# Four weight units of a mixer converted during attention, on one Trainium2 core

## The chip, the cores and the metric

One core of one Trainium2 chip runs the whole program. The metric is the device time of one execution in microseconds (us), as the median of several runs. The engines named below are PE (TensorE matmul), DVE (VectorE), ACT (ScalarE), POOL (GpSimd) and SP, which here only issues DMAs.

## What is computed

A clustered attention (2 batches, 8 heads, 768 positions, 64 wide; a query sees a key only if both fall to the same of 16 centroids of its head) feeds two mixers in a row:

```python
x = attention(q, k, v, centroids)              # 2 x 768 x 512
u = x + (x^T @ U @ V)^T                        # first mixer, rank 32
x = u + relu(u @ w_ch1) @ w_ch2                # w_ch1 512 x 2048, w_ch2 2048 x 512
h = relu(x^T @ w_tok1) @ w_tok2                # second mixer
u = x + h^T
out = u + relu(u @ w_ch1') @ w_ch2'            # 1536 wide
```

The weights arrive as 64-bit floats and are used as a pair of 32-bit parts (a high one that the fast matmul takes exactly, and the rest), so each product is three matmuls.

## The kernel before

**Attention** runs in 96 steps (function step, lines 643 to 693), one tile of 128 queries each. Step n issues the score matmuls of tile n+2, DVE's maximum over them (s_max, line 289), ACT's exponential of tile n+1 (s_exp, line 294), PE's transposes of tile n (line 311), their copies out of PSUM by ACT and DVE in turn (lines 318 and 316), and the product with v. Other work is hung on steps by two tables: mid, which runs before the exponential, and late, which runs at the end of the step. The late table holds the preparation of the next pair of heads: at step s1-8 its load, at s1-5 to s1+2 its scores, the cluster choice (arg0, arg2 and arg4 on DVE, arg1, arg3, k_lo and mask_rows on POOL, q_lo on DVE), where s1 is a multiple of 12. PE's transposes and several small products share three PSUM banks in turn (ring, line 301).

**Units.** The first mixer's channel weights come as NFA = 16 units of 1 MB of 64-bit numbers (a slice of w_ch1 and one of w_ch2). The function wide (line 490) converts unit k in stages numbered d: 1 loads it (SP, line 494), 3 takes the magnitude (ACT, line 96), 4, 4.5, 5 and 5.5 are four DVE operations on 1024 columns (lines 100, 103, 106, 109), 6 rounds the high part (ACT), 6.5 subtracts for the low part (DVE for the first ND = 6 units, POOL for the others), and 7 stores 1 MB to a scratch array in DRAM (SP, line 513 or 522). Two raw buffers alternate, so the load of a unit waits for stage 5.5 of the unit two before it.

**The schedule of the conversion.** Units 0 to 3 begin during attention, by the hand-written table early (line 628). The rest runs in ticks: tick n does stage d of unit k where 2k + int(d) = n (conv_all, line 555); after the 16 units follow 31 smaller blocks (narrow) for the second mixer.

**The mixer** runs in slots (half_slots, line 797). Slot 2k+1 issues hidden(k+1), 12 matmuls of 512 columns with the first half of a unit, slot 2k+2 issues outmm(k), 12 with the second half; between them ACT and DVE make gh and gl (lines 728 and 729). Each unit serves four passes over the tokens, the first two interleaved by the cuts 0, 6, 11, 16: units 0 to 5 for pass 0, then for pass 1, then units 6 to 10 for both, then 11 to 15. The weights stand in three buffers (whl), and the function feed (line 704) fetches a half (512 KB) from the scratch array, for every place from the seventh on, four slots before its use: slot 2u-5 fetches the first half for place u, used in slot 2u-1, and slot 2u-2 the second half, used in slot 2u+2. Below, F12 is the fetch issued in slot 12.

Before each slot the main loop steps two generators, rest_of_u and conv_rest (line 894); the latter decides whether the slot gets a tick:

```python
if k + NTICK < 2 * ND + 5 or k % 9 % 2 or k % 9 == 0:
    tick()
```

so slots 0 to 7 have one tick each, and from slot 8 on five slots of nine have one (9, 10, 12, 14, 16, 18, 19, 21, 23 and so on). All loads, stores and fetches are issued by SP in the order in which the program names them, and one that has to wait holds back those behind it.

Of the kernel before, what the change touches and what calls it, by code (L numbers as in the profile page):

```python
# [10 lines left out]
F32R = mybir.dt.float32r  # L11
# [7 lines left out]
P = 128  # L19
# [5 lines left out]
def tile_cluster_attention__then__two_mixers(  # L25
# [32 lines left out]
    NFA, NFB = wa.shape[0], wb.shape[0]  # L58
# [25 lines left out]
    def sub(eng, o, a, b):  # L84
        eng.tensor_tensor(out=o, in0=a, in1=b, op=ALU.subtract)  # L85
# [3 lines left out]
    def conv(dst, raw):  # L89


        w = raw.bitcast(I32).rearrange("p (n two) -> p n two", two=2)
        lo, hi, d = w[:, :, 0], w[:, :, 1], dst.bitcast(I32)

        def magnitude():
            act.activation(dst, hi.bitcast(F32), AF.Abs)  # L96

        def clamp():

            dve.tensor_scalar(out=dst, in0=dst, scalar1=2.0 ** -15, scalar2=122879.9921875, op0=ALU.max, op1=ALU.min)  # L100

        def shift():
            dve.tensor_scalar(out=d, in0=d, scalar1=3, scalar2=0x3FFFFFF8, op0=ALU.logical_shift_left, op1=ALU.bitwise_and)

        def low_bits():
            dve.scalar_tensor_tensor(out=d, in0=lo, scalar=29, in1=d, op0=ALU.logical_shift_right, op1=ALU.bitwise_or)  # L106

        def top_bits():
            dve.scalar_tensor_tensor(out=d, in0=hi, scalar=-0x40000000, in1=d, op0=ALU.bitwise_and, op1=ALU.bitwise_or)  # L109

        return [magnitude, clamp, shift, low_bits, top_bits]
# [5 lines left out]
    ND = cuts[1]  # L117
# [13 lines left out]
    w64 = [c64_[:, ts(i, 1024)] for i in range(2)]  # L131
    w32 = [c32_[:, ts(i, 1024)] for i in range(2)]
    u0 = [qk0[:, ts(i, 2048)].rearrange("p (c n) -> p c n", c=NC) for i in range(2)]
    chl = [qk1[:, ts(4 + i, 1024)].rearrange("p (h n) -> p h n", h=2) for i in range(2)]
# [3 lines left out]
    ap = ap_ctx.enter_context(tc.tile_pool(name="ap", bufs=1))  # L138
# [22 lines left out]
    pt = ap.tile([P, 4 * NBL * P], F32, name="pt")  # L161
    osb = [ap.tile([P, HS], F32, name=f"osb{i}") for i in range(2)]
    nm = ap.tile([P, 4], F32, name="nm")
    rs = [ap.tile([P, 2 * NT], F32, name=f"rs{i}") for i in range(4)]
    rr = [ap.tile([P, 2 * NT], F32, name=f"rr{i}") for i in range(2)]

# [315 lines left out]
    blocks = []  # L482
# [4 lines left out]
            blocks.append((wt2[ts(c, P), ts(h, HS)].unsqueeze(1), None, (c, h)))  # L487
    blocks += [(wb[f][:, ts(i, 512)], scr[1][f, i], None) for f in range(NFB) for i in range(2)]

    def wide(k, d):  # L490
        r64, r32 = w64[k % 2], w32[k % 2]
        ops = conv(r32, r64)
        if d == 1:
            sp.dma_start(r64, wa[k])
        elif d == 3:
            ops[0]()
        elif d == 4:
            ops[1]()
        elif d == 4.5:
            ops[2]()  # L500
        elif d == 5:
            ops[3]()
        elif d == 5.5:
            ops[4]()
        elif k < ND:
            o, r = whl[k % NW], r32.rearrange("p (i n) -> p i n", i=2)
            if d == 6:
                rnd(act, o[:, :, 0, :], r)
            elif d == 6.5:
                sub(dve, o[:, :, 1, :], r, f32(o[:, :, 0, :]))  # L510
            else:
                for i in range(2):
                    sp.dma_start(scr[0][k, i], f32(o[:, i]).rearrange("p h n -> p (h n)"))
        else:
            for i in range(2):
                o, r = chl[2 * (k % 2) + i], r32[:, ts(i, 512)]
                if d == 6:
                    rnd(act, o[:, 0, :], r)
                elif d == 6.5:
                    sub(pool, o[:, 1, :], r, f32(o[:, 0, :]))  # L520
                else:
                    sp.dma_start(scr[0][k, i], f32(o).rearrange("p h n -> p (h n)"))
# [30 lines left out]
            sp.dma_start(dst, f32(chl[k % 2]).rearrange("p h n -> p (h n)"))  # L553

    def conv_all():
        for n in range(NTICK, 2 * NFA + len(blocks) + 8):
            for d in (7, 6, 5, 5.5, 1, 4, 4.5, 3, 6.5):
                k, r = divmod(n - int(d), 2)
                if r == 0 and 0 <= k < NFA:
                    wide(k, d)  # L560
            for d in (5, 4, 3, 2, 0):
                k = n - 2 * NFA - 2 - d
                if 0 <= k < len(blocks):
                    narrow(k, d)
            yield

    cgen = conv_all()

    def tick():
        next(cgen, None)  # L570
# [4 lines left out]
    mid, late = {}, {}  # L575

    def at(d, s, f):
        d.setdefault(max(s, 0), []).append(f)

    for g in range(G):  # L580
        s0 = NTT * g
        for h in range(2):
            s = s0 + 2 * NT * h + 4 * NT + 1
# [5 lines left out]
        n, s1 = g + 1, s0  # L589
# [20 lines left out]
    for t in range(NS):  # L610
        s = (59, 63, 69, 75, 81, 87)[t]
# [12 lines left out]
    for i, s in ((0, 6), (1, 11)):  # L624
        for k in range(5):
# [2 lines left out]
    early = [(56, 0, 1), (57, 1, 1), (60, 0, 3), (61, 0, 4), (63, 0, 4.5), (65, 0, 5), (67, 0, 5.5), (68, 2, 1), (69, 1, 3),  # L628
             (70, 1, 4), (72, 1, 4.5), (74, 1, 5), (76, 1, 5.5), (77, 3, 1), (82, 0, 6), (83, 0, 6.5), (85, 0, 7),
             (84, 2, 3), (87, 2, 4), (89, 2, 4.5), (93, 1, 6), (94, 1, 6.5)]  # L630
    for s, k, d in early:
        at(late, s, lambda k=k, d=d: wide(k, d))
    NTICK = 9
    for t in range(TW // P):

# [256 lines left out]
    end = lambda m, p: 2 * (NFA * (p + 1) if m == 0 else NFA * NPASS + NFB * (p + 1)) + 1  # L892

    def conv_rest():
        for k in range(3 * (2 * NFA + len(blocks))):
            if k + NTICK < 2 * ND + 5 or k % 9 % 2 or k % 9 == 0:
                tick()
            yield

    bg = [rest_of_u(), conv_rest()]  # L900
    while done < end(0, 2) - 24:
        for t in bg:
# [48 lines left out]
```

## Time and profile before

| what | value |
|---|---|
| median of 3 runs | 796.47 us (795.81 to 799.31) |
| profiled execution | 796.2 us |
| its span, first to last instruction | 794.1 us |
| mean granted clock of TensorE | 0.999 |
| busy in the span: PE, DVE, ACT, POOL | 96%, 62%, 38%, 20% |
| DMA | 176.66 MB, 222 GB/s over the span |

Attention takes the span up to about 280 us, the mixers the rest. A window of the trace gives, for each engine, the time it was busy and its number of instructions, and the share of the 16 DMA engines in use. A busy PE is not always a PE at its peak, since matmuls overlap and their ends are modelled.

### The profile page before, as it was taken

How to read it: one execution, taken by the hardware profiler on the slowest of the kernel's cores; microseconds unless marked ns; L12 is line 12 of the kernel's file. 1: busy time of each engine (PE TensorE's matmuls, PEld its weight loads, DVE VectorE, ACT ScalarE, POOL GpSimd, SP SyncE). 2: the span in 40 equal slices, each digit the busy share in tenths (PEclk: the TensorE clock that was granted, in tenths of full speed). 3: DMA queues.
4: the chain of work that ended last, by engine and by line, in shares of the span. 5: the costliest groups of instructions: out<-in, count | busy, mean ns of one | idle time of the engine just before them, and what ended most of it. 6: DMA issues, size and time to landing. Idle time of an engine off the chain costs nothing.

```text
span 794.1 us, 10612 instructions
## 1 busy us (share of the span) xinstructions
PE 760.7 (96%) x3845; PEld 584.4 (74%) x3845; DVE 488.4 (62%) x719; ACT 305.6 (38%) x563; POOL 156.5 (20%) x135
## 2 busy tenths in 40 slices
PE   1989999999999999899999999999999999999998
PEld 0655666666666677677788888888888888888886
DVE  5877767768877589695757887856682232114113
ACT  3566665666666444232323333323241210110110
POOL 3340430421400001141322222214411220000000
PEclk9999999999999999999999999999999999999999
DMA  5962644566621158999999899978775437555752
GB/s 148 214 128 81 139 113 129 126 207 152 165 92 54 54 212 292 392 368 353 391 386 326 302 392 375 377 282 277 267 282 206 134 133 246 203 187 169 273 193 80
DMA packets 59204, 176.66 MB, mean 222 GB/s; under 512 B 8625, under 2 KB 16817, under 8 KB 57105
## 3 DMA queue, kind: packets, MB, share of 16 engines
q1 hardware_dynamic: 58640, 175.27, 66.0%
q10 hardware_dynamic: 512, 0.72, 0.3%
q8 instruction: 30, 0.49, 0.2%
q14 instruction: 22, 0.17, 0.1%
HBM read 124.58 MB, written 32.51 MB: 198 GB/s over the span
## 4 chain that ended last, share of the span: by engine, by line
PE 86%; DMA 6%; DVE 3%; ACT 2%; issue 1%; ACTq 0%; SPq 0%; DVEq 0%
PE ps L73 76%; PE ps L311 8%; DMA qk<-scr_a 4%; PE ps L331 1%; DMA sk__80<-in_kT_dram 1%; DVE c__75 L106 1%; PE ps L823 1%; DVE c__75 L109 1%; DMA sq__79<-in_qT_dram 1%; ACT qk L78 1%; DMA qk<-sq__79 0%; PE ps L368 0%; ACT p L294 0%; DMA qk<-om 0%; DVE gl L729 0%
## 5 line engine op out<-in xcount | busy, mean ns | idle before, releaser
L73 PE MATMUL ps<-gh,qk 128*128 128x512 f32 x672 | 221.8, 391 | 3.3 <-DMA qk<-scr_a 3.2
L729 DVE SCALAR_TENSOR_TENSOR gl<-ps,gh 128x512 fp32r<-128x512 f32 x84 | 58.0, 690 | 190.7 <-ACT gh L728 190.7
L728 ACT ACTIVATE gh<-ps 128x512 fp32r<-128x512 f32 x84 | 50.2, 598 | 274.6 <-PE ps L73 274.1
L73 PEld LDWEIGHTS ps<-gh,qk 128*128 128x128 f32 x672 | 126.2, 188 | 30.6 <-ACT c__75 L96 2.7
L73 PE MATMUL ps<-qk 112*128 112x384 f32 (+2 forms) x492 | 119.6, 371 | 12.1 <-DMA qk<-om 9.7
L73 PE MATMUL ps<-gl,qk 128*128 128x512 f32 x336 | 130.9, 390 | 0.0
L289 DVE TENSOR_REDUCE nm<-ps 128x1 f32<-128x768 f32 x96 | 91.7, 955 | 41.0 <-PE ps L73 39.5
L73 PEld LDWEIGHTS ps<-qk 112*128 112x128 f32 (+1 forms) x492 | 84.6, 192 | 37.3 <-ACT p L294 14.3
L311 PEld LDWEIGHTS ps<-ident,p 128*128 128x128 f32 x576 | 67.0, 141 | 35.4 <-issue 19.3
L85 POOL TENSOR_TENSOR qk<-c__75,qk 128x512 fp32r<-128x512 f32 x34 | 49.1, 1449 | 222.9 <-ACT qk L78 220.3
L311 PE MATMUL ps<-ident,p 128*128 128x128 f32 x576 | 89.5, 278 | 2.4 <-ACT p L294 1.5
L294 ACT ACTIVATE p<-ps,nm 128x768 f32<-128x768 f32 x96 | 86.6, 902 | 11.2 <-DVE nm L289 10.6
L73 PE MATMUL ps<-pt,vr 128*64 128x384 f32 x384 | 82.1, 510 | 0.0
L73 PE MATMUL ps<-u1h,qk 128*128 128x512 f32 x224 | 73.9, 391 | 0.1
L73 PE MATMUL ps<-u2h,qk 128*128 128x512 f32 x224 | 73.9, 391 | 0.0
L73 PEld LDWEIGHTS ps<-gl,qk 128*128 128x128 f32 x336 | 63.1, 188 | 12.5
L318 ACT COPY pt<-ps 128x512 f32<-128x512 f32 x72 | 42.1, 585 | 70.7 <-PE ps L311 69.3
L73 PE MATMUL ps<-qk,qk 128*128 128x512 f32 x228 | 55.9, 394 | 1.0 <-DMA qk<-scr_a 1.0
L73 PEld LDWEIGHTS ps<-qk,qk 128*128 128x128 f32 x228 | 42.2, 188 | 10.0 <-DMA qk<-scr_a 1.4
L316 DVE COPY pt<-ps 128x512 f32<-128x512 f32 x72 | 49.0, 681 | 0.4 <-PE ps L311 0.4
L73 PEld LDWEIGHTS ps<-u1h,qk 128*128 128x128 f32 x224 | 42.0, 188 | 9.1 <-DMA qk<-scr_a 0.5
L73 PEld LDWEIGHTS ps<-u2h,qk 128*128 128x128 f32 x224 | 42.0, 188 | 8.6
(138 smaller groups left out, 906.9 us busy)
## 6 DMA issues: line engine op xcount, KB each, us to landing
qk<-scr_a SPq DMA_DIRECT2D x84, 512.0 KB, 7.9
qk<-scr_b SPq DMA_DIRECT2D x72, 512.0 KB, 4.2
c__74<-in_wa_dram SPq DMA_DIRECT2D x16, 1024.0 KB, 6.2
c__74<-in_wb_dram SPq DMA_DIRECT2D x24, 512.0 KB, 6.7
scr_b<-qk SPq DMA_DIRECT2D x24, 512.0 KB, 6.5
scr_a<-qk SPq DMA_DIRECT2D x22, 512.0 KB, 4.9
qk<-sq__79 SPq DMA_DIRECT2D x14, 384.0 KB, 4.0
qk<-sk__80 SPq DMA_DIRECT2D x28, 192.0 KB, 2.8
```

What stands on the lines that cost most here:

```text
L73: pe.matmul(o, lhsT=l, rhs=r, start=start, stop=stop, **kw)
L78: act.activation(o, i, AF.Copy, scale=scale)
L85: eng.tensor_tensor(out=o, in0=a, in1=b, op=ALU.subtract)
L106: dve.scalar_tensor_tensor(out=d, in0=lo, scalar=29, in1=d, op0=ALU.logical_shift_right, op1=ALU.bitwise_or)
L109: dve.scalar_tensor_tensor(out=d, in0=hi, scalar=-0x40000000, in1=d, op0=ALU.bitwise_and, op1=ALU.bitwise_or)
L289: dve.tensor_reduce(out=nm[:, n % 4 : n % 4 + 1], in_=ps[:, b0 : b0 + 2, 0:HS], axis=AX.XY, op=ALU.max, negate=True)
L294: act.activation(p32[n % NP32].rearrange("p (j k) -> p j k", j=2), ps[:, b0 : b0 + 2, 0:HS], AF.Exp, bias=nm[:, n % 4 : n % 4 + 1], accum_ ...
L311: pe.transpose(ps[:, tb[j], ts(i, P)], p32[n % NP32][:, ts(c, P)], ident)
L316: dve.tensor_copy(o, ps[:, tb[j], :])
L318: act.copy(o, ps[:, tb[j], :])
L728: act.activation(gh, o, AF.Relu)
L729: dve.scalar_tensor_tensor(out=gl, in0=o, scalar=0.0, in1=f32(gh), op0=ALU.max, op1=ALU.subtract)
```

## The change

Units 6 to 9 are now converted during attention, one after another, and get four small output buffers (echl: two for each of two alternating units) in the memory of attention. The index of wide becomes a place in a new order: 6, 7, 8, 9, then 0 to 5, then 10 to 15. The stages of these four units are hung on the late table from steps 19, 28, 38 and 47: load six steps earlier, then one stage in each step, and the store eight steps after. The ticks count 12 units in place of 16, and the slots that have one are others: 0 to 7 all, up to 23 three of four (9, 10, 11, 13, 14, 15, 17, 18, 19, 21, 22, 23), then every odd one.

```diff
+    echl = [ap.tile([P, 2, 512], F32R, name=f"echl{i}") for i in range(4)]
...
-    def wide(k, d):
-        r64, r32 = w64[k % 2], w32[k % 2]
+    NE = 4
+    order = [*range(ND, ND + NE), *range(ND), *range(ND + NE, NFA)]
+    NWA = NFA - NE
+
+    def wide(n, d):
+        k = order[n]
+        r64, r32 = w64[n % 2], w32[n % 2]
...
-                o, r = chl[2 * (k % 2) + i], r32[:, ts(i, 512)]
+                o, r = (echl if n < NE else chl)[2 * (n % 2) + i], r32[:, ts(i, 512)]
...
-        for n in range(NTICK, 2 * NFA + len(blocks) + 8):
+        for n in range(NTICK, 2 * NWA + len(blocks) + 8):
...
-                if r == 0 and 0 <= k < NFA:
-                    wide(k, d)
+                if r == 0 and 0 <= k < NWA:
+                    wide(NE + k, d)
...
-                k = n - 2 * NFA - 2 - d
+                k = n - 2 * NWA - 2 - d
...
+    for k, s in enumerate((19, 28, 38, 47)):
+        for d, i in ((1, -6), (3, 0), (4, 1), (4.5, 2), (5, 3), (5.5, 4), (6, 5), (6.5, 6), (7, 8)):
+            at(late, s + i, lambda k=k, d=d: wide(k, d))
     for s, k, d in early:
-        at(late, s, lambda k=k, d=d: wide(k, d))
+        at(late, s, lambda k=k, d=d: wide(NE + k, d))
...
-        for k in range(3 * (2 * NFA + len(blocks))):
-            if k + NTICK < 2 * ND + 5 or k % 9 % 2 or k % 9 == 0:
+        for k in range(3 * (2 * NWA + len(blocks))):
+            if k < 8 or (k < 4 * ND and k % 4) or k % 2:
```

The changed kernel's lines are numbered 1 higher from line 164 on, 6 from the body of wide on and 9 after the tables. Two places show how instructions move.

DVE in attention, steps 20 to 24. The maximum writes nm, the copy out of PSUM writes pt, amx and ohT belong to the cluster choice (arg0, arg2, arg4), c__75 is the converted unit, and sq__79 is written by q_lo. Before:

```order
L203 TENSOR_REDUCE amx<-am_81 128x24
L289 TENSOR_REDUCE nm<-ps 128x1
L316 COPY pt<-ps 128x512
L289 TENSOR_REDUCE nm<-ps 128x1
L316 COPY pt<-ps 128x512
L216 TENSOR_REDUCE amx<-am_82 128x24
L289 TENSOR_REDUCE nm<-ps 128x1
L316 COPY pt<-ps 128x512
L289 TENSOR_REDUCE nm<-ps 128x1
L226 STREAM_TRANSPOSE ohT<-am_83 128x384
L238 SCALAR_TENSOR_TENSOR sq__79<-sq__79 128x768
```

In the changed kernel, the same steps, as far as the fourth conversion operation (the maximum and the rows of arg4 and q_lo follow it):

```order
L204 TENSOR_REDUCE amx<-am_81 128x24
L100 TENSOR_SCALAR c__75<-c__75 128x1024
L290 TENSOR_REDUCE nm<-ps 128x1
L317 COPY pt<-ps 128x512
L103 TENSOR_SCALAR c__75<-c__75 128x1024
L290 TENSOR_REDUCE nm<-ps 128x1
L317 COPY pt<-ps 128x512
L217 TENSOR_REDUCE amx<-am_82 128x24
L106 SCALAR_TENSOR_TENSOR c__75<-c__74,c__75 128x1024
L290 TENSOR_REDUCE nm<-ps 128x1
L317 COPY pt<-ps 128x512
L109 SCALAR_TENSOR_TENSOR c__75<-c__74,c__75 128x1024
```

One conversion operation now stands ahead of each of four maxima in a row, beside the work on the next pair of heads.

SP's queue in the mixer, from the fetches of slot 9 on. c__74 is the raw unit that is loaded, scr_a the scratch array, qk the weight buffers (as a target of a fetch) or the converted parts (as the source of a store, like xnl). Before:

```order
L712 DMA qk_73<-scr_a 128x1024
L712 DMA qk_72<-scr_a 128x1024
L712 DMA qk_73<-scr_a 128x1024
L522 DMA scr_a<-qk_73 128x1024 x2
L494 DMA c__74<-in_wa_dram 128x1024
L712 DMA qk_73<-scr_a 128x1024
L712 DMA qk_72<-scr_a 128x1024
L712 DMA qk_73<-scr_a 128x1024 x2
L522 DMA scr_a<-xnl 128x1024 x2
L494 DMA c__74<-in_wa_dram 128x1024
```

In the changed kernel:

```order
L721 DMA qk_73<-scr_a 128x1024
L721 DMA qk_72<-scr_a 128x1024
L528 DMA scr_a<-qk_73 128x1024 x2
L500 DMA c__74<-in_wa_dram 128x1024
L721 DMA qk_73<-scr_a 128x1024 x2
L721 DMA qk_72<-scr_a 128x1024
L528 DMA scr_a<-xnl 128x1024 x2
L500 DMA c__74<-in_wa_dram 128x1024
L721 DMA qk_73<-scr_a 128x1024 x2
L721 DMA qk_72<-scr_a 128x1024
```

The first store and load that stood behind F9, F10 and F11 now stand ahead of F11, the next ones behind three fetches in place of four. After the load of slot 17 no full unit is loaded any more, while in the kernel before the last one is loaded in slot 34.

## Rows read from the trace of the kernel before

**Rows 1.** The page, its first part: busy time of each engine over the span.

```profile
PE 760.7 (96%) x3845; PEld 584.4 (74%) x3845; DVE 488.4 (62%) x719; ACT 305.6 (38%) x563; POOL 156.5 (20%) x135
```

**Rows 2.** Windows: start:end, length, busy of PE, PEld, DVE, ACT, POOL, clock, DMA, GB/s.

```profile
330.30:384.00 53.70, 51.25 (x226) 41.49 (x226) 36.77 (x48) 15.60 (x25) 15.83 (x10) 1.00 0.98 376
400.00:420.00 20.00, 20.00 (x94) 16.56 (x93) 11.22 (x21) 5.80 (x11) 3.62 (x4) 1.00 1.02 393
```

**Rows 3.** Waits of PE from 235 to 420 us: total, times, longest.

```profile
PE ps L73 <- DMA qk<-scr_a: 4.7, 4, 2.3
```

**Rows 4.** The chain that ended last, from 270 to 420 us: start, length, what.

```profile
319.50 1.24 DVE c__75 L109
...
320.75 0.33 SPq L494
...
321.17 9.14 DMA qk<-scr_a
```

**Rows 5.** Waits of SP's DMA queue from 270 to 420 us.

```profile
SPq L494 <- DVE c__75 L109: 51.8, 12, 11.6
```

**Rows 6.** Timeline of SP, 310 to 346 us: start, length, what.

```profile
313.57 0.33 SPq L494 DMA_DIRECT2D c__74<-in_wa_dram  x1
```

**Rows 7.** Timeline of PE, 313 to 385 us: first matmuls of slots 15, 16, 21, 29, 34.

```profile
325.27 0.39 PE L73 MATMUL ps<-u1h,qk 128*128 128x512 f32 x1
...
330.45 0.47 PE L73 MATMUL ps<-gh,qk 128*128 128x512 f32 x1 [2.29 <-DMA qk<-scr_a]
...
344.38 0.39 PE L73 MATMUL ps<-u1h,qk 128*128 128x512 f32 x1
...
369.02 2.88 PE L73 MATMUL ps<-qk 128*128 128x512 f32 x12
...
384.14 0.47 PE L73 MATMUL ps<-gh,qk 128*128 128x512 f32 x1 [0.87 <-DMA qk<-scr_a]
```

**Rows 8.** Windows: 80 us of attention without any conversion.

```profile
100.00:180.00 80.00, 80.00 (x502) 52.26 (x502) 55.57 (x86) 49.71 (x101) 21.52 (x20) 1.00 0.55 142
```

**Rows 9.** The chain in attention: the same place of three rounds of 12 steps.

```profile
142.29 1.70 PE ps L73 x8
...
173.39 1.70 PE ps L73 x8
...
204.91 1.92 PE ps L73 x9
```

**Rows 10.** Groups on DVE up to 275 us: the conversion of units 0 to 2.

```profile
L106 DVE SCALAR_TENSOR_TENSOR c__75<-c__74,c__75 128x1024 int32<-128x1024 int32 x2 | 2.4, 1216 | 0.0
...
L103 DVE TENSOR_SCALAR c__75<-c__75 128x1024 int32<-128x1024 int32 x3 | 2.0, 682 | 0.0
```

**Rows 11.** Timeline of DVE, 78 to 94 us: four maxima, in brackets the idle time before.

```profile
81.89 0.96 DVE L289 TENSOR_REDUCE nm<-ps 128x1 f32<-128x768 f32 x1 [0.65 <-PE ps L73]
...
84.42 0.96 DVE L289 TENSOR_REDUCE nm<-ps 128x1 f32<-128x768 f32 x1 [0.51 <-PE ps L73]
...
86.56 0.96 DVE L289 TENSOR_REDUCE nm<-ps 128x1 f32<-128x768 f32 x1 [0.58 <-PE ps L73]
...
89.09 0.96 DVE L289 TENSOR_REDUCE nm<-ps 128x1 f32<-128x768 f32 x1 [0.25 <-PE ps L73]
```

**Rows 12.** Timeline of ACT, 84 to 94 us: the exponential behind the second of them.

```profile
85.97 0.91 ACT L294 ACTIVATE p<-ps,nm 128x768 f32<-128x768 f32 x1
```

**Rows 13.** Timeline of PE, 81 to 96 us: the transposes that read it, from the third on.

```profile
87.62 0.66 PE L311 MATMUL ps<-ident,p 128*128 128x128 f32 x4
```

**Rows 14.** Groups on DVE from 312 to 400 us, where POOL works too.

```profile
L103 DVE TENSOR_SCALAR c__75<-c__75 128x1024 int32<-128x1024 int32 x9 | 13.0, 1448 | 0.3
```

**Rows 15.** Timeline of POOL, 76 to 92 us: k_lo.

```profile
86.05 1.82 POOL L85 TENSOR_TENSOR sk__80<-sk__80 128x768 fp32r<-128x768 f32 x1
```

**Rows 16.** Timeline of SP, 96 to 98 us: the load of the next pair.

```profile
97.11 0.58 SPq L178 DMA_DIRECT2D sq__79<-in_qT_dram  x1
```

**Rows 17.** Timeline of PE around 105 us: the scores that need that load.

```profile
104.88 0.52 PE L73 MATMUL ps<-sq__79,zc 128*32 128x384 f32 x2
```

## Prediction, made before the changed kernel ran

> **What bounds the kernel now.** I first read the page: PE is busy for 760.7 of 794.1 us [rows 1], so only some 33 us are open at all, and most of these lie in the setup, which the change leaves alone. The waits of PE from 235 to 420 us show what the change can reach: four waits for a weight fetch, together 4.7 us [rows 3]. That is the most that better feeding can win. About 0.5%, or 4.0 us, is what a measurement of this kernel can tell from no change.
>
> Then I read why the fetches are late. The windows show the DMA engines 98% busy between 330 and 384 us at 376 GB/s, and 102% at 393 GB/s right after [rows 2]. The queue is full, not merely slow to react. The chain adds a second cause: the load of a unit waits for the last DVE operation of an older one, and a fetch behind it on SP goes out only at 321.17 and lands 9.14 us later [rows 4]. SP spends 51.8 us in such waits [rows 5]. After 400 us the DMA is as full, yet PE does not wait. So lateness needs both: a full queue, and fetches held back by a unit's load.
>
> In attention PE is busy for 80 of 80 us, DVE for 55.57, ACT for 49.71 and POOL for 21.52, with the DMA engines at 55% [rows 8]. PE bounds it; DVE has some room on average.
>
> **The change, in the mixer.** Four units (8 MB of traffic) leave it. The first nine slots stay as they were, though, and from slot 9 to 23 the ticks become denser, three of four slots for five of nine. So I count what the queue has to move before a given fetch. I count in halves of 512 KB (0.524 MB); one takes 1.39 us at 376 GB/s or 1.33 at 393 [rows 2]; a load or a store of a unit is two halves.
>
> From the load issued at 313.57 [rows 6] the changed queue holds load, F9, F10, store, load, F11: nine halves. Before, F12 was the tenth half in this list, and it landed at 321.17 + 9.14 = 330.31 [rows 4]. The same ten halves are moved in another order, so F11 lands one half earlier, at about 328.9. Its user, slot 15, was ready at 325.27 [rows 7]: a wait of 3.7 us, where slot 16 waited 2.29 before. F12 then is in time, since slot 16 has moved by as much.
>
> From there on, F17 is 13 halves later: F13, store, load, F14, F15, F16, store, load, F17. It lands at 330.3 + 13 x 1.33 = 347.6 (348.4 at the slower rate). Its slot 21 began at 344.38 [rows 7] with 2.29 us of wait behind it, so at 342.1 without; all waits together must then be 5.5 (6.3) us. F25 is 30.75 halves after F12 (three more stores, seven fetches and 3.75 halves of small blocks lie between F18 and it): 371.2 (373.0). Its slot 29 began at 369.02 [rows 7] after 4.7 - 0.9 = 3.8 us of waits, so at 365.2 without: 6.0 (7.8) us. Later the queue gets lighter, for ticks of small blocks come only every second slot, and these do not hold fetches back. I take 5.7 us of waits in all, between the two at the faster rate, since with no unit to load after slot 17 the queue runs as it does after 400 us. Against 4.7 that is **+1.0 us**. The ends are 3.7 (only F11 late: -1.0) and 7.8 (+3.1). The gain in traffic comes after slot 25, where nothing waited for it except slot 34's 0.87 us [rows 7].
>
> **The change, in attention.** Each unit adds four DVE operations, in four steps running: 2 x 0.68 + 2 x 1.22 = 3.8 us (L100 taken as long as L103, L109 as L106) [rows 10]. In unit 0's stretch, four maxima in a row leave DVE 0.65 + 0.51 + 0.58 + 0.25 = 2.0 us idle [rows 11]. So DVE falls 1.8 us behind. How late may a maximum be? The one at 84.42 ends at 85.38, its exponential starts at 85.97 [rows 12], 0.59 later, ends at 86.88, and the transposes that read it begin with the third of four from 87.62, at about 87.9 [rows 13], 1.0 later: 1.6 us of slack. Alone, then, the four operations cost 0.2 us.
>
> They do not run alone. Where POOL works, L103 takes 1448 ns on average in place of 682 [rows 14, 10], 0.77 more, and in unit 0's four steps POOL runs the choice of clusters and k_lo (1.82 us) [rows 15]. I take two such hits: 1.8 + 1.5 - 1.6 = **+1.7 us** for unit 0. The Trainium skill (SBUF — State Buffer, Who interferes with whom) speaks against this placement: VectorE and GpSimd share a pair of ports, and an instruction that needs it waits until the other engine's whole instruction has ended. By that rule two hits of a full k_lo would be 3.6 us and unit 0 would cost 3.8; the trace shows longer operations, and mostly a part of such a wait. Units 1 to 3 I cost at nothing: unit 2 has no preparation in its four steps, and in units 1 and 3 only one operation falls beside POOL, so the 1.6 us of slack covers them; with that cover gone they cost what unit 0 does. The ends for attention are 0 and 4 x 1.7 = 6.8 us. For the low end: from 142.29 to 173.39 twelve steps take 31.10 us, and from there to 204.91, with four conversion operations spread over every second step, 31.52 [rows 9], of which two added products explain most. Spread out, a unit is free.
>
> ACT (one magnitude and two roundings) and POOL (two subtractions, each no longer than k_lo) are costed at nothing: ACT idles 38% and POOL 73% of attention [rows 8]. On SP, three issues per unit of 0.33 us [rows 6] fall among those of the next pair. Unit 0's two stores now stand ahead of a pair's load: 2.7 us of DMA. That load is issued at 97.11 [rows 16] and its scores start at 104.88 [rows 17]; 7.8 us leave room for 2.7 more.
>
> **Sum.** 796.2 us (the profiled execution) + 1.0 + 1.7 = **798.9 us**. The median of the runs shown is 0.3 above the profiled one, too little to move the forecast. It stays within 0.5%.
>
> **The rivals.**
> - The feeding is cured (chance 0.12). Fewer units in the mixer might free SP early enough that no fetch is late. For it: the last full unit is loaded in slot 17. Against it: the first nine slots are unchanged, and F11 now stands behind one more load. It gives 796.2 - 4.7 = 791.5 if attention is free, 793.2 with unit 0's 1.7; I put a third of the chance below 792.5.
> - Slower (0.22). DVE falls behind in every unit, because each has at least two operations beside POOL's and all meet the maximum. It decides once DVE is more than 1.6 us late in two units besides unit 0. At 1.7 us each: 796.2 + 1.0 + 6.8 = 804.0. The port rule of the Trainium skill page named above is this mechanism; rows 14 bear it out in size, and no row of attention shows it.
> - Nothing moves (0.08). Attention hides all, and the waits stay 4.7 us, only at other slots: 796.2.
>
> The forecast has 0.58, with its own range of 796.5 to 801.5; a sixth of that or a little less lies above 800.5. So **faster** has 0.04, **slower** 0.22 + 0.06 = 0.28 and **the same** 0.68. The range for 8 in 10 leaves out the first rival's better part and the worst of the second: **794.0 to 803.5**.
>
> **What would show it.** In the changed profile: a wait of PE for a fetch of about 3.7 us near 325 us plus the shift, in place of the one of 2.29; waits for fetches of 5 to 6 us in all, and none after slot 30; DVE's L103, L106 or L109 longer than 0.7 or 1.3 us near 80 us, and a gap of one or two us in PE there, but none in the other three stretches. Waits for fetches under 2 us in all would prove the mixer's step wrong; gaps in attention at all four units, or at none, the step on unit 0.

## The result, and the profile after

The changed kernel takes **801.63 us** (median of 9 runs, 799.81 to 802.73), the kernel before 797.28 us on the same chip (9 runs, 794.54 to 799.31). The ratio is 1.0052 with an interval of 1.0035 to 1.0068: slower by 4.2 us by the ratio and 4.35 by the medians. So it is slower, and whether by more than the 0.5% that the prediction took for the least that can be told stays undecided, for the interval holds that bound. The profiled execution took 800.52 us, its span 798.5, 4.4 more than before.

The page's first part, for the changed kernel, beside [rows 1]:

```profile
PE 763.1 (96%) x3845; PEld 585.3 (73%) x3845; DVE 481.6 (60%) x719; ACT 304.8 (38%) x563; POOL 154.2 (19%) x135
```

No engine got more instructions. PE is busy for 2.4 us more, of which 1.7 are one slow slot of the mixer (below); the rest of the loss is waiting. To find where, I compared the start of the same exponential of ACT and of the same slot of PE in the two traces. A step n in the table is the exponential of tile n, which runs near the end of step n-1. The shift over the kernel before, in us:

| place | shift | gained or lost since the last |
|---|---|---|
| steps 14 and 22 (setup behind, no unit yet on DVE) | -0.53 | (setup) |
| step 28 (unit 0's four DVE operations) | +0.14 | 0.67 lost |
| step 34 (the pair load behind unit 0's stores) | +1.49 | 1.35 lost |
| step 40 (unit 1, POOL) | +2.54 | 1.05 lost |
| step 52 (unit 2, which cost nothing up to step 46, then unit 3's DVE operations) | +2.78 | 0.24 lost |
| step 60 (the next pair load but one) | +3.56 | 0.78 lost |
| step 95 and slot 1 of the mixer | +3.57 | 0 |
| slot 36 | +4.83 | 1.26 lost |
| the end | +4.42 | 0.41 gained, at slots 66 and 67 |

Attention lost 4.1 us, where the prediction had 1.7. The mixer lost 0.85, where it had 1.0. But the last row says nothing of the change: all thirteen other traces gain about 0.4 us at slots 66 and 67 against this one trace of the kernel before, with the old ticks too. Up to slot 36 the mixer had lost 1.26. Three places of attention show how.

**The pair load.** SP's issue of the pair's second half in the kernel before (start, length, what), which follows the row in [rows 16]:

```profile
97.73 0.43 SPq L179 DMA_DIRECT2D sk__80<-in_kT_dram  x1
```

SP's timeline in the changed kernel, from 98 to 101 us, then PE's from 105 to 107, as [rows 17] before:

```profile
98.57 1.00 SPq L528 DMA_DIRECT2D scr_a<-echl  x2
99.62 0.78 SPq L179 DMA_DIRECT2D sq__79<-in_qT_dram  x1
100.45 1.17 SPq L180 DMA_DIRECT2D sk__80<-in_kT_dram  x1
```

```profile
105.49 0.84 PE L73 MATMUL ps<-sq__79,zc 128*32 128x384 f32 x4 [0.39 <-ACT p L295]
106.41 0.84 PE L73 MATMUL ps<-sk__80,zc 128*32 128x384 f32 x4
```

The tile view of sk__80 from 96 to 112 us gives the time from its issue to its landing, first of the kernel before, then of the changed one:

```profile
DMA to landing us min/median/max: 3.9/3.9/3.9
```

```profile
DMA to landing us min/median/max: 5.9/5.9/5.9
```

Before, sk__80 was issued at 97.73 and landed at 101.6, 3.3 us ahead of its use at 104.9 (right behind the row in [rows 17]). Now it is issued at 100.45, lands at 106.4, and PE takes it at once. The load comes 4.7 us later (4.6 without the 0.14 that the steps themselves had lost); 3.3 of that was covered, the other 1.3 is the loss at step 34.

**Unit 1 on POOL.** POOL from 112 to 126 us, DVE in the same stretch, and PE's gap:

```profile
116.13 2.52 POOL L85 TENSOR_TENSOR echl<-c__75,echl 128x512 fp32r<-128x512 f32 x2
118.60 0.84 POOL L85 TENSOR_TENSOR am<-am,amx 128x384 bf16<-128x384 bf16 x1
119.53 1.17 POOL L222 TENSOR_SCALAR am<-am 128x384 bf16<-128x384 bf16 x1
120.67 1.82 POOL L85 TENSOR_TENSOR sk__80<-sk__80 128x768 fp32r<-128x768 f32 x1
```

```profile
120.73 0.58 DVE L227 STREAM_TRANSPOSE ohT<-am 128x384 bf16<-128x384 bf16 x1 [0.63 <-POOL am L222]
121.24 2.07 DVE L239 SCALAR_TENSOR_TENSOR sq__79<-sq__79 128x768 fp32r<-128x768 f32 x1
123.23 0.94 DVE L290 TENSOR_REDUCE nm<-ps 128x1 f32<-128x768 f32 x1
```

```profile
124.83 0.66 PE L312 MATMUL ps<-ident,p 128*128 128x128 f32 x4 [0.86 <-DVE pt L317]
```

The two subtractions stand ahead of arg3 (the next two rows) on POOL. DVE's arg4 waits 0.63 us for arg3. Then q_lo (L239), behind it, meets k_lo (POOL's last row) and takes 2.07 us; in the rows of the kernel with POOL's work moved, below, it takes 1.12. The maximum at 123.23 stands behind both. q_lo ends at 123.31, 0.82 behind k_lo's end at 122.49; in that other kernel it meets only the last 0.31 us of k_lo and ends 0.81 behind it. So both times it looks as if it had begun about when k_lo ended; undisturbed, in the kernel before, it takes 0.92. The Trainium skill (SBUF — State Buffer, Who interferes with whom) says that an operation of VectorE with two inputs in SBUF contends with one of GpSimd that reads SBUF, and that whichever issues first keeps the other out for its whole instruction; these two traces agree.

**Unit 0 on DVE.** The second to fourth conversion operations (DVE), and two operations of POOL in the same steps:

```profile
80.95 0.68 DVE L103 TENSOR_SCALAR c__75<-c__75 128x1024 int32<-128x1024 int32 x1
...
83.49 1.22 DVE L106 SCALAR_TENSOR_TENSOR c__75<-c__74,c__75 128x1024 int32<-128x1024 int32 x1
...
86.09 1.21 DVE L109 SCALAR_TENSOR_TENSOR c__75<-c__74,c__75 128x1024 int32<-128x1024 int32 x1
```

```profile
83.65 1.75 POOL L85 TENSOR_TENSOR am<-am,amx 128x384 bf16<-128x384 bf16 x1 [0.67 <-DVE amx L217]
...
86.62 2.37 POOL L85 TENSOR_TENSOR sk__80<-sk__80 128x768 fp32r<-128x768 f32 x1
```

DVE's operations keep the lengths of [rows 10]. It is POOL that was held up: 1.75 us, where the same operation takes 0.84 in the kernel before, and 2.37 for 1.82 [rows 15]. So the two hits of 0.77 that the prediction put on DVE fell on the other engine. That they did no more there than make k_lo, and the stacks that need it, later is read from the rows; no run takes unit 0 alone out of this place.

**The mixer.** Waits of PE from 235 to 420 us, as [rows 3], and first matmuls of slots 13, 15 and 16, as [rows 7]:

```profile
PE ps L73 <- DMA qk<-scr_a: 4.7, 3, 3.2
```

```profile
323.71 0.50 PE L73 MATMUL ps<-u1h,qk 128*128 128x512 f32 x1 [0.55 <-DMA qk<-scr_a]
...
332.60 0.50 PE L73 MATMUL ps<-u1h,qk 128*128 128x512 f32 x1 [3.16 <-DMA qk<-scr_a]
...
337.04 0.40 PE L73 MATMUL ps<-gh,qk 128*128 128x512 f32 x1
```

F11 is late: PE waits 3.16 us for it at slot 15, after 0.55 at slot 13 for an earlier fetch. Against a slot 15 that had not waited before, that is 3.7, as predicted. The chain from 305 to 336 us names the queue, as [rows 4] did:

```profile
322.26 1.23 DVE c__75 L109
...
323.52 0.33 SPq L500
...
323.94 8.61 DMA qk<-scr_a
```

The row that nobody expected is the length of slot 15: from 332.60 to 337.04, 4.44 us for twelve matmuls that take 2.72 elsewhere. The windows show why (the columns are those of [rows 2]; the granted clock is the third number from the right):

```profile
332.00:335.00 3.00, 2.40 (x7) 1.97 (x8) 2.42 (x2) 1.56 (x3) 1.83 (x2) 0.73 1.03 419
335.00:338.00 3.00, 3.00 (x11) 2.31 (x11) 0.13 (x1) 0.60 (x1) 1.14 (x1) 0.70 1.04 436
340.00:360.00 20.00, 20.00 (x90) 16.56 (x89) 16.72 (x21) 6.10 (x9) 6.50 (x4) 1.00 1.03 412
```

After the wait, the clock stood at the lower of its two levels, 1.2 GHz, for most of that slot. The late F17 and F25 of the prediction do not show: the only other wait is 0.94 us, at slot 27, where the kernel before waits 0.98. In all PE waits 4.7 us for fetches, as before.

### The profile page after: what moved, and what is told of

It is laid out like the page before. It is cut to its first block, busy times and chain, and to the rows that moved or that the text cites. A ratio compares the mean times of both kernels' runs of the same rounds, so it can differ in the third digit from the quotient of the medians.

```text
span 798.5 us, 10596 instructions
## 1 busy us (share of the span) xinstructions
PE 763.1 (96%) x3845; PEld 585.3 (73%) x3845; DVE 481.6 (60%) x719; ACT 304.8 (38%) x563; POOL 154.2 (19%) x135
## 4 chain that ended last, share of the span: by engine, by line
PE 83%; DVE 6%; DMA 5%; ACT 2%; issue 1%; POOL 1%; SPq 1%; ACTq 0%; DVEq 0%; POOLq 0%
PE ps L73 74%; PE ps L312 7%; DMA qk<-scr_a 2%; DMA sk__80<-in_kT_dram 2%; DVE c__75 L106 1%; DVE c__75 L109 1%; PE ps L332 1%; DMA qk<-sk__80 1%; PE ps L832 1%; ACT p L295 1%; DMA sq__79<-in_qT_dram 1%; ACT qk L78 1%; DVE qk L85 0%; DVE gl L738 0%; PE ps L369 0%
## 5 line engine op out<-in xcount | busy, mean ns | idle before, releaser
L85 POOL TENSOR_TENSOR qk<-c__75,qk 128x512 fp32r<-128x512 f32 x30 | 41.0, 1371 | 209.9 <-ACT qk L78 205.3
```

## The experiments

All kernels but one (the new rate alone) are edits of the changed one; the last three are edits of the aligned one, and the last two of these have the thinner ticks as well. Losses at steps and slots are always against the one trace of the kernel before, read as in the table above. The setup differs between executions, by up to 4.0 us at step 14 (where it was latest, the granted clock was 0.86 from 45 to 60 us), whatever the kernel. So losses are counted from step 14 on, and a median can lie well below the profiled time. The mixer differs too: in the four traces whose mixer is the changed kernel's (that one, stores later, load earlier and POOL later) slots 1 to 36 lost 1.26, 0.35, 1.07 and 1.72 us. In attention the same loss comes back to within 0.02 us at units 0, 1 and 3, but not at the pair loads.

**Half rate.** Every second slot has a tick from slot 8 on.

```diff
-            if k < 8 or (k < 4 * ND and k % 4) or k % 2:
+            if k < 8 or k % 2:
```

> Theory (the dense ticks of slots 9 to 23 cost the mixer its gain): with a tick only every second slot from slot 8 on, F11 no longer stands behind a second load and store. From the load at 313.57 us, F13 is then the eleventh half and lands near 331.7, about 1 us after its slot would start. So the waits of PE for fetches are 0 to 1.5 us in all instead of 4.65, the granted clock stays at 1.0 from 325 to 345 us, and hidden(8) takes 2.7 us and not 4.4. The mixer gains 3.2 to 4.7 us on waits and 1.7 us on the clock: about 5 us less than the changed kernel, that is 1 us faster than before (796). Attention still ends 3.6 us late. Rival (the queue is full whatever the rate, since F11 to F25 are late for the bytes of the whole stretch): waits of 4 to 5 us in all at other slots, 801 to 802 us.

Measured: 795.83 us, ratio 0.9972 (0.9952 to 0.9992). The waits of PE from 235 to 420 us, and the window from 330 to 340 us:

```profile
PE ps L73 <- DMA qk<-scr_a: 1.4, 2, 1.2
```

```profile
330.00:340.00 10.00, 8.83 (x39) 7.02 (x38) 6.13 (x7) 3.35 (x5) 3.52 (x2) 1.00 1.01 388
```

The waits fell to 1.4 us, the clock stayed at 1.0, and from slot 1 to 36 the mixer took 4.2 us less than before. Attention lost 4.7, 1.1 more than expected. For the mixer the theory holds in its numbers, and the rival falls: the bytes are the same in all, and the pace decides.

**Old rate.** The four units stay in attention, the ticks have the rate of before.

```diff
-            if k < 8 or (k < 4 * ND and k % 4) or k % 2:
+            if k + NTICK < 2 * ND + 5 or k % 9 % 2 or k % 9 == 0:
```

> The four units stay in attention and the ticks get the rate of before (five slots of nine from slot 8 on). Theory (the clock fell because PE stood idle for 3.16 us at once, and that came from the dense ticks): F12 is again the late fetch, with a wait of about 2.3 us, as in the kernel before; the clock stays at 1.0; the later waits are gone or under 1 us each, because units end at about slot 25. Waits of 2.3 to 3.5 us in all: the mixer takes 1 to 2.5 us less than before, and with attention's 3.6 us the whole is 1 to 2.6 us slower than before (798 to 800). Rival (the clock falls whenever PE waits for a fetch in this stretch, or it falls for another reason, such as the load of PE ahead): hidden(8) or outmm(7) takes over 4 us here too, and the whole is 800 to 802 us.

Measured: 799.08 us, ratio 1.0021 (1.0003 to 1.0039), as expected. The waits of PE from 235 to 420 us:

```profile
PE ps L73 <- DMA qk<-scr_a: 3.0, 2, 2.2
```

The clock stayed at 1.00 from 320 to 360 us. From slot 1 to 36 the mixer took 2.2 us less than before. So moving four units is worth 2.2 us by itself, and the denser ticks give up 3.5.

**The new rate alone.** The kernel before, with the new rule and nothing in attention.

```diff
-            if k + NTICK < 2 * ND + 5 or k % 9 % 2 or k % 9 == 0:
+            if k < 8 or (k < 4 * ND and k % 4) or k % 2:
```

> The kernel before (all sixteen units in the mixer's stretch, none in attention) with the new rate of ticks. Theory (the dense ticks alone make F11 late and let PE's clock fall): a wait for F11 of 3 to 4 us at slot 15 with the clock at half right after it (hidden(8) in over 4 us), and more late fetches up to slot 30, since more units follow: 6 to 8 us of waits, 3 to 5 us slower than before, ratio 1.004 to 1.006. Rival (the rate does no harm by itself; the loss in the mixer comes with attention's late end): waits of 4.7 us as before, ratio 0.999 to 1.001.

Measured: 801.77 us, ratio 1.0051 (1.0035 to 1.0067); the waits from 235 to 420 us:

```profile
PE ps L73 <- DMA qk<-scr_a: 9.0, 5, 3.2
```

Attention is where it was to 0.1 us; from slot 1 to 36 the mixer took 5.8 us more. The ratio is the expected one, the waits are 1 us above the theory's, and the clock is as it said (0.83 from 330 to 340 us). With that the mixer from slot 1 to 36 can be read as a table (us against before):

| | ticks of before | the change's ticks | half rate |
|---|---|---|---|
| all units in the mixer | 0 | +5.8 | not run |
| four units in attention | -2.2 | +1.3 | -4.2 |

The differences within a row are larger than the 1.4 us by which one mixer differs between traces.

**Stores later.** Unit 0's stores at step 30, unit 2's at 51, unit 3's at 57.

```diff
+            i += {(0, 7): 3, (2, 7): 5, (3, 7): 2}.get((k, d), 0)
             at(late, s + i, lambda k=k, d=d: wide(k, d))
```

> The stores of units 0, 2 and 3 go to later steps (27 to 30, 46 to 51, 55 to 57), behind the load of the next pair and behind the stacks. Theory (the stores ahead of the pair load on SP and on the DMA engines delay the scores of two pairs): the wait of the scores near 105 us (1.5 us) and the gap near 170 us go, so attention ends 2.1 us earlier than in the changed kernel (1.34 + 0.78), and the mixer stays as it is: 799.5 us. Rival (the scores are late because DVE and POOL are late in the unit ahead, and the stores only stand beside it): attention ends at most 0.5 us earlier, 801 to 802 us.

Measured: 800.42 us, ratio 1.0025 (1.0010 to 1.0040). The time lies between the two sides (799.5 and 801), and the trace gives each a half: at step 34, 1.24 us were still lost, while the loss at step 60 was gone. SP's timeline from 94 to 104 us shows what was left:

```profile
95.41 0.55 SPq L266 DMA_DIRECT2D qk<-om  x1
97.79 0.51 SPq L267 DMA_DIRECT2D qk<-om  x1
...
103.00 1.46 SPq L180 DMA_DIRECT2D sk__80<-in_kT_dram  x1
```

The pair load was issued 2.7 us late with no store ahead of it. SP stood still from 96.0 to 97.79. Unit 1's load was issued at 90.58 and took 7.2 us to land (the tile view of c__74, 88 to 100 us):

```profile
DMA to landing us min/median/max: 7.2/7.2/7.2
```

It landed at 97.78, and the eighth issue after it went out at 97.79. In the profile of the changed kernel, too, that issue (94.05) follows the landing (88.05 + 5.9 = 93.95). So that load holds SP back by its own transfer time. The traces show the rule behind it: SP's 467 issues carry eight semaphores, nearly always in turn, and in all 14 traces none goes out before the DMA that last had its semaphore has landed. The prediction had overlooked it, and the next runs test what it costs.

**Load earlier.** Only unit 1's load moves, from step 22 to 17.

```diff
+            i += {(1, 1): -5}.get((k, d), 0)
             at(late, s + i, lambda k=k, d=d: wide(k, d))
```

> Only unit 1's load moves, from step 22 (between the two parts of the stacks) to step 17; unit 0's stores stay ahead of the pair load. Runs so far show PE losing 1.2 to 2.6 us at the scores near 105 us, and 1.2 even with the stores behind the pair load, where the pair load was still issued 2.7 us late, after SP had waited for unit 1's load to land (97.79 behind 97.78 us). Theory (the load is the larger part, the stores the smaller): the pair load is issued about 1 us later than in the kernel before, its second half lands near 104.5 us, and the loss at the scores is 0 to 0.5 us; attention ends about 2 us earlier than with the load in its place, and the whole takes about 799.7 us. Rival (the stores decide, the load only delays transfers that nobody waits for): the loss stays at 1.2 us or more.

Measured: 802.70 us, ratio 1.0053 (1.0037 to 1.0070). The expectation was wrong: 1.47 us were lost at step 34, as the rival had it. SP in that stretch, and the tile view of sk__80 from 98 to 112 us:

```profile
100.27 1.00 SPq L528 DMA_DIRECT2D scr_a<-echl  x2
...
102.15 1.17 SPq L180 DMA_DIRECT2D sk__80<-in_kT_dram  x1
```

```profile
DMA to landing us min/median/max: 6.5/6.5/6.5
```

The step is 2.36 us late in this execution, so sk__80 lands at 102.15 + 6.5 - 2.36 = 106.3, 4.7 us later than in the kernel before; 4.7 - 3.3 of cover is 1.4. The stores cost more than their issues and the 2.7 us of transfer that I had taken.

**All four moves and the half rate.** Stores, load, POOL (as in the next run) and the ticks together.

```diff
+            i += {(0, 7): 3, (1, 1): -5, (1, 6.5): 4, (1, 7): 4, (2, 7): 5, (3, 7): 2}.get((k, d), 0)
             at(late, s + i, lambda k=k, d=d: wide(k, d))
...
-            if k < 8 or (k < 4 * ND and k % 4) or k % 2:
+            if k < 8 or k % 2:
```

> The load of unit 1 at step 17, the stores of units 0, 2 and 3 at 30, 51 and 57, unit 1's subtractions and stores at 38 and 40, and a tick every second slot from slot 8 on: all four edits together. Theory (each repairs its own loss, and the losses add): attention keeps only unit 0's 0.5 us on DVE and unit 3's 0.25 us, the mixer gains 4.2 us as with the half rate alone: 3.4 us less than before, ratio 0.9955 to 0.9965. Rival (in attention the queues shift the losses elsewhere): attention ends 2 us or more late and the ratio is 0.998 or more.

Measured: 793.35 us, ratio 0.9941 (0.9924 to 0.9958), a little more gain than expected, though the interval reaches the expected 0.9955. SP, and the tile view of sk__80, in the same place:

```profile
103.16 0.43 SPq L180 DMA_DIRECT2D sk__80<-in_kT_dram  x1
```

```profile
DMA to landing us min/median/max: 3.6/3.6/3.6
```

With neither the load nor the stores ahead, the pair lands in 3.6 us and nothing is lost at step 34 (at most 0.01 us). Each of the two alone makes sk__80 some 4.5 to 4.7 us late, 1.2 to 1.5 more than the 3.3 of cover; both in place cost 1.35, 2.59, 2.23, 2.37 and 1.94 us in the five traces that have them. So either is enough for a loss, and in the changed kernel's own trace the two cost no more than one. Attention lost 0.9 us in all: unit 0's 0.68 and unit 3's 0.24. The mixer gained 4.3.

**POOL later.** Unit 1's subtractions at step 38, its stores at 40.

```diff
+            i += {(1, 6.5): 4, (1, 7): 4}.get((k, d), 0)
             at(late, s + i, lambda k=k, d=d: wide(k, d))
```

> Unit 1's two subtractions on POOL and its stores go four steps later (34 to 38, 36 to 40), behind the choice of clusters. Theory (these 2.5 us stand ahead of arg3 on POOL, arg4 on DVE waits for arg3, and the maxima queue behind arg4 and a blocked q_lo): the gap of PE near 125 us (0.86 us) goes, and the step of the score matmuls there by 1.0 to 1.1 us; attention ends about 1 us earlier, 800.6 us. Rival (DVE is overloaded in every unit by its own four operations): the gap stays at 0.6 us or more and the time at 801 to 802.

Measured: 801.05 us, ratio 1.0045 (1.0027 to 1.0063). The time alone would not tell it from the changed kernel (step 34 lost 2.37 here), but the trace does: from step 34 to 40 nothing is lost, in place of 1.05 to 1.07 in the six other traces that keep the place. DVE's arg4 and q_lo there, for the rows above:

```profile
121.79 0.57 DVE L227 STREAM_TRANSPOSE ohT<-am 128x384 bf16<-128x384 bf16 x1
122.28 1.12 DVE L239 SCALAR_TENSOR_TENSOR sq__79<-sq__79 128x768 fp32r<-128x768 f32 x1
```

arg4 no longer waits. The rival (DVE overloaded by its own four operations) falls for unit 1.

**Filler.** The changed kernel with 13 matmuls ahead of hidden(8), whose results are not used.

```diff
+        if k == 8:
+            for _ in range(13):
+                mm(o, whl[7 % NW][:, 0, 0, 0:P], fst["u"][p][0][:, 0, :], True, True)
```

> The changed kernel with 13 more matmuls of 512 columns ahead of hidden(8), on weights that are there already, into the bank that hidden(8) then starts anew; the results are not used. They take 2.95 us at the 0.227 us of the 12 matmuls of a slot and so fill the 3.16 us for which PE waits for F11. Theory (the granted clock falls because PE stands idle): the clock stays at 1.0 from 330 to 340 us, hidden(8)'s own 12 matmuls take 2.7 and not 4.4 us, and from slot 16 on the kernel is about 1.7 us earlier than the changed one, set against the start of the mixer: 800 us. Rival (the clock falls for another reason, at this time or with this traffic): the clock is 0.83 in that window as before and the time is 801 to 803.

Measured: 802.71 us, ratio 1.0055 (1.0041 to 1.0069). Windows, PE's rows (filler, hidden(8), slot 16), and the waits from 235 to 420 us:

```profile
330.00:335.00 5.00, 4.29 (x20) 3.22 (x19) 2.94 (x4) 2.15 (x3) 0.38 (x1) 1.00 1.00 378
335.00:340.00 5.00, 5.00 (x24) 4.10 (x23) 3.58 (x4) 0.60 (x2) 2.61 (x2) 1.00 1.03 425
```

```profile
330.31 3.11 PE L73 MATMUL ps<-u1h,qk 128*128 128x512 f32 x13
334.13 0.50 PE L73 MATMUL ps<-u1h,qk 128*128 128x512 f32 x1 [0.70 <-DMA qk<-scr_a]
...
337.02 0.39 PE L73 MATMUL ps<-gh,qk 128*128 128x512 f32 x1
```

```profile
PE ps L73 <- DMA qk<-scr_a: 2.4, 4, 0.8
```

Half of each side came true. PE did not stand idle, the clock stayed at 1.00, and hidden(8) took 2.89 in place of 4.44 us: the clock falls behind the idle time. But the time did not fall. Counted from slot 1, slot 16 starts 0.8 us earlier than in the changed kernel, and slot 29 at the same 87.75 us in both. In between, PE lost 0.51 us at slot 18 and 0.50 at slot 29 against the changed kernel, and smaller amounts at five others, though it was spared the 0.94 of slot 27. This fits fetches that set the pace: the slow slot 15 then used up time that PE would have waited anyway.

**Aligned.** Units at steps 13, 25, 37, 49, so that DVE's four operations fall into steps 2 to 5 of each twelve, POOL's into 7, load and stores into 6 and 8, with the half rate.

```diff
-    for k, s in enumerate((19, 28, 38, 47)):
-        for d, i in ((1, -6), (3, 0), (4, 1), (4.5, 2), (5, 3), (5.5, 4), (6, 5), (6.5, 6), (7, 8)):
+    for k, s in enumerate((13, 25, 37, 49)):
+        for d, i in ((1, -7), (3, 0), (4, 1), (4.5, 2), (5, 3), (5.5, 4), (6, 5), (6.5, 6), (7, 7)):
...
-            if k < 8 or (k < 4 * ND and k % 4) or k % 2:
+            if k < 8 or k % 2:
```

> The units in attention start at steps 13, 25, 37 and 49, so that their four DVE operations fall into steps 2 to 5 of each twelve, where no preparation of a pair runs, POOL's subtractions into step 7, ahead of the cluster choice, the load into step 6 and the stores into step 8, both behind the pair load of step 4; a tick every second slot from slot 8 on. Theory (a unit costs nothing where DVE, POOL and SP are free, as unit 2 of the changed kernel did): attention ends 0 to 0.6 us late, the mixer gains 4.2 us: 3.6 to 4.2 us less than before, ratio 0.9945 to 0.9955. Rival (DVE's four operations in a row are too much for any stretch): about 1.7 us per unit, attention 5 us or more late, ratio over 1.0.

Measured: 792.17 us, ratio 0.9929 (0.9908 to 0.9949). Units 1 to 3 cost nothing (the shift is 1.27 us from step 22 to 60), so four DVE operations in a row are not too much in free steps. Unit 0, in the steps where the setup still splits V, cost 0.9. PE's long gap there is not its doing, for the kernel before (first row) has it as well; in both, ACT's exponential stands behind 2.54 us of that split:

```profile
71.02 0.44 PE L311 MATMUL ps<-ident,p 128*128 128x128 f32 x2 [1.53 <-ACT p L294]
```

```profile
71.89 0.44 PE L312 MATMUL ps<-ident,p 128*128 128x128 f32 x2 [1.49 <-ACT p L295]
```

New in the aligned kernel are two shorter ones:

```profile
67.59 0.99 PE L73 MATMUL ps<-qk 112*128 112x384 f32 x4 [0.24 <-ACT p L295]
...
74.58 0.55 PE L332 MATMUL ps<-ident,osb 128*128 128x128 f32 x3 [0.31 <-DVE pt L317]
```

The first waits for an exponential whose maximum DVE began at 65.57, right behind the unit's second operation (64.97), and the second for a copy behind its fourth (71.83). Behind the third (66.43) no new gap shows.

**Aligned, thinner ticks.** Two slots of five until slot 32.

```diff
+            if k < 8 or (k < 34 and k % 5 in (0, 2)) or (k > 34 and k % 2):
```

> The aligned units, and the ticks still thinner: two slots of five from slot 10 to 32, then every second one from slot 35. With two fifths the queue has to move nine halves in five slots, 12.3 us at 376 GB/s for 13.3 us of PE, so it catches up. Theory: the one wait for a fetch that the aligned kernel has left (0.8 us at slot 17) goes, none comes in its place, 0.8 us less than the aligned kernel: ratio 0.991 to 0.993. Rival (the small blocks end later and the second mixer waits for its weights): a wait of PE later than 450 us, ratio 0.993 or more.

Measured: 791.67 us, ratio 0.9916 (0.9904 to 0.9927). No wait for a fetch is left between 235 and 800 us; from slot 1 to 36 the mixer took 5.9 us less than before (the aligned kernel 5.0, a difference within the spread of one mixer over several traces). The small blocks did not come late.

**Unit 0 shifted** (the aligned kernel with the thinner ticks; unit 0's last two DVE operations come a step later, the rest at 26, 27 and 29).

```diff
+            i += {5: 1, 5.5: 1, 6: 8, 6.5: 8, 7: 9}.get(d, 0) if k == 0 else 0
```

> As the aligned kernel with the thinner ticks, but unit 0, which alone cost 0.9 us there (its third DVE operation at step 16 made a maximum late, an exponential waited for it, and PE stood 1.49 us), has its last two DVE operations one step later (17 and 18), its rounding and subtractions at steps 26 and 27 and its stores at 29. Theory (attention then loses at most 0.3 us from step 14 to 22): 0.6 us less than the kernel with unit 0 in place. Rival (the stretch is bound by the split of V on ACT and any operation there costs): the same time as that kernel.

Measured: 792.76 us, ratio 0.9930 (0.9915 to 0.9945). It missed: from step 14 to 22, 1.6 us were lost, more than with the unit in place. Neither side foresaw that. The expectation had taken the gap of 1.49 us for unit 0's doing, and so moved the third operation, behind which no new gap shows, and the fourth with it. The trace shows what came of it: DVE idles 2.87 us for ACT's part of the split, until 72.20, and both moved operations now stand behind it, at 73.18 and 75.79. PE waits 0.32 and 0.37 us for copies behind them and 1.71 in place of 1.53 in the long gap; the 0.24 stays. No run tests this account.

**Three units.** Of the aligned kernel with the thinner ticks, the unit at step 13 goes back to the mixer.

```diff
-    NE = 4
+    NE = 3
...
-    for k, s in enumerate((13, 25, 37, 49)):
+    for k, s in enumerate((25, 37, 49)):
```

> The aligned kernel with the thinner ticks, but three units in attention (6, 7, 8 at steps 25, 37 and 49) in place of four: the one at step 13, which alone cost 0.9 us, is converted in the mixer again. Theory (the mixer's waits depend on how densely the ticks stand in slots 8 to 23, not on one unit more): attention ends within 0.2 us of the kernel before, no wait for a fetch over 0.5 us comes in its place, and the whole takes 0.7 to 1.0 us less than with four units: ratio 0.990 to 0.991. Rival (the fourth unit is what keeps the queue free): waits for fetches of 1 us or more between slots 16 and 40, or late weights of the second mixer, and a ratio of 0.992 or more.

Measured: 791.36 us, ratio 0.9897 (0.9880 to 0.9913). Attention lost 0.01 us, the mixer took 6.0 us less than before, with no wait for a fetch. The interval overlaps that of four units, but the trace shows the 0.9 us: the fourth unit is not needed. Both versions beat the kernel before and the changed one.

## Why the prediction was right, and where wrong

The range of 794.0 to 803.5 held the time, and the likeliest case, no change that can be told, stands on the edge: 0.52% where the bound is 0.5, with an interval on both sides of it. The forecast of 798.9 was 1.6 us short of the profiled 800.52: it had 2.7 us of loss, where the profiled executions differ by 4.3. That the time fell into the range is in part luck. Two places that were costed at nothing, SP's queue and POOL, took 3.2 us; 1.0 too much on unit 0, and a setup that happened to be 0.5 us shorter, hid some of it. By its own steps:

- **The mixer, +1.0: measured +0.85,** or +1.26 up to slot 36, without the 0.4 that seems to belong to the one trace of before. F11's 3.7 us were right to 0.1. F17 and F25 were not late in the changed kernel, and the waits did not grow: PE had lost another 1.7 us in slot 15 to its clock. The filler run removes that and brings small losses at slots 18 to 29 instead, with nearly the same sum (+1.28 up to slot 36). So the queue's arithmetic was right in the sum; that PE's clock would fall was not foreseen, and by the filler run it cost nothing here. Other traces of the same mixer give 0.35 to 1.72, so that the last tenths agree is luck.
- **Unit 0, +1.7: measured 0.67.** The two hits of 0.77 were put on DVE. They fell on POOL, and the longer operations on DVE that were to show it did not come. Without them the prediction's own sum is 0.2; q_lo's 1.23 us in place of 0.92 (80 to 90 us) adds 0.3, and the last 0.2 has no account.
- **SP and the pair load, at nothing: measured 1.35 (1.35 to 2.6 over the runs with the same places), and 0.78 at the next but one (0.1 to 0.8).** This is the step that failed: "7.8 us leave room for 2.7 more". The 7.8 run from the first issue to the use; the second half is issued 0.6 later and needs 3.9 to land, so the room was 3.3. And the delay was 4.7, not 2.7: the stores cost their issues (1.0) and SP's later stacks beside the transfer, and unit 1's load, which the step did not count at all, held SP until it had landed. At the next but one the room was 2.6 (landed at 164.54, used at 167.10 in the kernel before), and there too the load landed only as PE took it, in all six traces with the stores in place.
- **POOL, at nothing: measured 1.05, in unit 1.** "POOL 73% of attention" idle is an average. The two subtractions stood ahead of arg3, for which DVE waits, and the maxima queue behind that. The prediction looked at what DVE's operations do to the maxima, and not at what DVE itself waits for.
- **Units 1 to 3 on DVE, at nothing:** right, but for unit 3's 0.24.
- **The slower rival** gave 804.0 through DVE being late in every unit. That is 3.5 above the profiled time: attention lost 4.1 us of its 6.8, and by another mechanism, for the larger losses came over SP and POOL. Against the feeding rival the prediction named F11's place behind one more load. That was the reason why it did not come; the half rate shows that most of it was to be had by the rule of the ticks alone (waits of 1.4 us), the thinner ticks in the aligned kernel that all of it was.
- **The chances:** a sixth of the 0.58 is about 0.10, not the 0.06 that went into "slower"; by the text's own fraction "slower" has 0.32 and "the same" 0.64.

What stays open: why the losses at the pair loads differ between executions with the units' steps there unchanged. At step 60 they were 0.6 to 0.8 us in three traces and 0.1 to 0.3 in three others. In these six sk__80 was issued 1.9 to 2.8 us late, and took 3.9 to 5.1 us to land in place of 3.7; why these times vary is not shown.

## What to carry to other kernels

Work that is moved under a bound engine costs by its place in each queue, and not by its busy time: of four units of the same kind, those in free steps cost 0.0 us and those beside a preparation 1 to 2 us, with their loads and stores. The cover of a transfer is counted from its landing to its use, and every issue ahead of it in its queue counts, loads among them. When work leaves a full queue, keep the pace or thin it; here a denser pace turned a gain of 2.2 us into a loss of 1.3, half the slots made it 4.2, and two of five, with the units in free steps, 5.9.

## What the runs showed of the hardware

- After PE had waited 3.16 us at once, its granted clock was 0.73 and 0.70 in the next two windows of 3 us, and twelve matmuls took 4.44 us in place of 2.72. In the four other traces with a wait of 3.2 to 3.5 us it was 0.83 from 330 to 340 us, as in this one. After waits of 2.2 to 2.3 us (before, and with the old rate) it stayed at 1.00. With PE kept busy by matmuls of no use, it stayed at 1.00 as well.
- One load of 1 MB on SP held back the eighth issue behind it until it had landed (97.79 after 97.78 us), although that issue waits for nothing that the load brings. The two carry the same semaphore, one of eight that SP's issues share; in 14 traces of 467 issues each, none went out before the last DMA with its semaphore had landed.
- Where DVE and POOL met, either could be the one that waits: k_lo took 2.37 us for 1.82 on POOL, q_lo 2.07 for 0.92 on DVE (before).
